# Four kv heads per tile instead of two in a one-token attention and MLP kernel

## The chip, the cores and the metric

The kernel runs on one core of one Trainium2 chip. The metric is device microseconds of one execution; the figure that counts is the median of the runs. A core has five engines with queues of their own: TensorE (PE, with its weight load PEld), VectorE (DVE), ScalarE (ACT), GpSimd (POOL) and SyncE (SP), which here issues nearly all transfers. Sixteen DMA engines move the data from HBM (the chip's main memory) to SBUF (on-chip, 128 partitions). TensorE writes to PSUM, eight banks of 128 partitions by 512 float32 elements.

## What is computed

One token `x` (576 values) passes through two branches that a gate mixes:

```python
# A: attention of 32 query heads on 16 kv heads, the last W = 4096 rows of the cache
q = (x @ wq).reshape(B, Sq, 32, 128).transpose(0, 2, 1, 3)
k = repeat(k_cache[:, :, Sk - W:, :], 2, axis=1)       # Sk = 32768
v = repeat(v_cache[:, :, Sk - W:, :], 2, axis=1)
p = softmax(einsum("bhqd,bhkd->bhqk", q, k) * 128**-0.5)
a = einsum("bhqk,bhkd->bhqd", p, v).transpose(0, 2, 1, 3).reshape(B, Sq, 4096) @ wo
# B: dense layer, F = 4608
b = gelu(x @ w1 + b1) @ w2 + b2
g = sigmoid((x * gate_w).sum(-1, keepdims=True))
out = g * a + (1 - g) * b
```

Everything is bfloat16 in HBM. Read are 16.8 MB of keys, 16.8 MB of values, 4.7 MB each of `wq` and `wo`, and 5.3 MB each of `w1` and `w2`: 53.6 MB in all. With one token, no datum is used twice.

## The kernel before

**Tiles of keys and values.** A tile holds two kv heads, interleaved on the partitions: head 2m on the even, head 2m + 1 on the odd partitions. Each partition holds 64 consecutive rows of its head, 16 KB in one piece (`load_kv`, L99; two transfers of 1 MB each, issued by SP). The pool `kv_pool` has six such buffers, used in turn by K tiles, V tiles and, at the end, the four groups of `w2`. A second pool of three buffers, `w_pool`, takes `wq` (two pieces), `w1` (three pieces) and `wo` (two).

**Units.** Work is counted in 16 units `h`. A unit is 32 chunks of a K tile, a chunk being the 128 rows that lie at one place of all partitions: half a tile. For each unit:

- `transposes(h, i)`, i from 0 to 7: four 128x128 matmuls with the identity turn four chunks (L233) into a PSUM tile `tp` (three banks, pool `ps_t`), and one copy puts them into `kT` (two buffers): VectorE at i = 0, 3, 6 (L242), ScalarE otherwise (L244).
- `scores(h, s)`, s = 0, 1: four matmuls of 512 columns, which run beside each other in four column groups of the array (L264). Their stationary columns are taken from `qz`, the queries of both heads padded with zeros. As a chunk mixes the keys of two heads, each query row also gets scores against the other head's keys.
- `values(h, i)`: four of them (i from 0 to 3, or 4 to 7) run side by side in four column groups (L340). Each has 32 stationary columns of `ez` (the probabilities, transposed, at zeros elsewhere) and 512 columns of V, and sums into `acc`.

**Softmax** (`softmax(b)`, L272) is made four times, for a block of four units each. `row_max` (L283) adds a mask that drops the scores against the other head and takes the maximum of each row; `turn_max` brings the maxima of a query together; `spread` gives them back to all rows and takes the exponential (L305); `put` transposes the probabilities (L313) and copies them into `ez` (eight VectorE copies, L318). `heads_out(b)` takes the four diagonal blocks out of `acc` (L352, L356) and turns the result (L363).

**Order.** It is written out by hand (a manual schedule: each engine takes its instructions in program order). The main loop (L547 to L585) runs over the units. In unit h, SP is given a K tile or a V tile, the transposes of unit h + 1 run, the scores of unit h between them, the steps of the last block's softmax one by one between these, and the values of unit h - 6. So up to the last block every softmax runs beside transposes and scores of the next. After the loop the last softmax runs between values (L596 to L612). `w1` is multiplied in three pieces (L452), its GELU spread over a unit (`gelu`, L462: `h_r`, nine `turn_h` with the small `hT` matmuls L479, and `act`).

**The end.** With all heads out, `ot`, `ow_ps`, `ow_m` and `ow` (L631 to L648) prepare the columns for `wo`. The blocks of four matmuls at L669 first go through `wo` (64 matmuls), then through the first three groups of `w2` (18 each), into `part`. L677 adds the bias; L688 sums the four column groups and the fourth group of `w2`, which is loaded in three pieces; L701 and L702 write the result.

**SP's queue.** SP issues in program order. A load waits for the buffer that it overwrites (the transposes or values that read it), and for the transfer eight issues earlier.

Of the kernel before, what the change touches and what calls it, by code (L numbers as in the profile page):

```python
# [16 lines left out]
def kernel(  # L17
# [24 lines left out]
    NCK = W // (P // 2)  # L42
    NCH = NCK // 2
    NU = 2 * (Hkv // 2)
# [19 lines left out]
    HB = 4  # L64
    NB = Hkv // HB
    R = 2 * HB
    RP = R // 2
    BC = 4
    NBL = NCH // BC
    NGR = 2 * NBL // NQ  # L70
    MASK = -1.0e30
# [5 lines left out]
    kv_pool = ctx.enter_context(tc.tile_pool(name="kv_pool", bufs=6))  # L77
# [20 lines left out]

    def load_kv(cache, m, name):  # L99
        t = kv_pool.tile([P, NCK, Dh], BF16, name=name, tag="kv")  # L100
        for e in range(2):
            nc.sync.dma_start(  # L102
                out=t[e:P:2],
                in_=cache[0, 2 * m + e, Sk - W : Sk, :].rearrange("(p c) d -> p c d", c=NCK),
            )
        return t
# [7 lines left out]
    WMAX = 36 * 256  # L114
# [17 lines left out]
    k_tiles[0] = load_k(0)  # L132
# [4 lines left out]
    for i in range(2):  # L137
        wq_t.append(load_flat(wq_flat, i * QP * QC, QP * QC, "wq_t"))

# [7 lines left out]
    qz = const.tile([P, Hkv // 2, 56], BF16, name="qz")  # L147
# [17 lines left out]
    for o in range(2):  # L165
# [21 lines left out]

    row_e = const.tile([P, 2], FP32, name="row_e")
    nc.vector.tensor_reduce(
        out=row_e[:], in_=ident_f[:].rearrange("p (a e q) -> p e a q", e=2, q=2), axis=AX.XY,  # L190
        op=ALU.add,
    )
    nc.vector.tensor_scalar(
        out=row_e[:], in0=row_e[:], scalar1=-MASK, scalar2=MASK, op0=ALU.mult, op1=ALU.add
    )
    mask = const.tile([P, BC * P], BF16, name="mask")
    for e in range(2):
        nc.vector.tensor_copy(
            out=mask[:, e::2], in_=row_e[:, e : e + 1].to_broadcast([P, BC * P // 2])
        )  # L200
# [27 lines left out]
    def transposes(h, i):  # L228
        if i == 0:
            kT[h] = kT_pool.tile([P, W], BF16, name="kT", tag="kT")  # L230
        tp = ps_t.tile([P, BC * P], FP32, name="tp", tag="tp")
        for c in range(BC):
            nc.tensor.matmul(  # L233
                tp[:, c * P : (c + 1) * P],
                lhsT=k_tiles[h // 2][:, (h % 2) * NCH + i * BC + c, :],
                rhs=ident[:],
                start=True,
                stop=True,
            )
        dst = kT[h][:, i * BC * P : (i + 1) * BC * P]  # L240
        if i in (0, 3, 6):
            nc.vector.tensor_copy(out=dst, in_=tp[:])  # L242
        else:
            nc.scalar.copy(out=dst, in_=tp[:])  # L244
# [4 lines left out]

    ez = const.tile([P, 2, HB // 2, 2 * NBL, BC, R], BF16, name="ez")  # L250
    nc.gpsimd.memset(ez[:].rearrange("p a b c d e -> p (a b c d e)"), 0.0)
# [4 lines left out]
    def scores(h, s):  # L256

        b, ul = h // HB, h % HB
        if ul == 0 and s == 0:
            s_tiles[b] = ps_s.tile([P, BC * P], FP32, name="s_ps", tag="s")  # L260
        lo = R * (NGR - 1 - 2 * (h % 2) - s)
        for t in range(NQ):
            i = 4 * s + t
            nc.tensor.matmul(  # L264
                s_tiles[b][32 * t : 32 * (t + 1), :],
                lhsT=qz[:, h // 2, lo : lo + 32],
                rhs=kT[h][:, i * BC * P : (i + 1) * BC * P],
                start=(ul == 0 and s == 0),
                stop=(ul == HB - 1 and s == 1),
            )  # L270

    def softmax(b):  # L272
# [3 lines left out]
        ms = small.tile([P, BC * P], FP32, name="ms", tag="ms")  # L276
        m8 = small.tile([1, R], FP32, name="m8", tag="m8")
# [4 lines left out]
        def row_max():  # L282
            nc.vector.tensor_tensor_reduce(  # L283
                out=ms[:], in0=s_ps[:], in1=mask[:], scale=1.0, scalar=-3.0e38,
                op0=ALU.add, op1=ALU.max, accum_out=mx[:],
            )

        def turn_max():
# [3 lines left out]
                out=m8[:], in_=mT[:].rearrange("o (s r) -> o r s", r=R), axis=AX.X, op=ALU.max  # L292
            )
            nc.vector.tensor_copy(
                out=m_all[:].rearrange("o (s r) -> o s r", r=R),
                in_=m8[:].rearrange("o (s r) -> o s r", s=1).to_broadcast([1, P // R, R]),
            )

        def spread():
# [6 lines left out]
                out=pr[:], in_=ms[:], func=ACT.Exp, bias=nb[:, 0:1], scale=SCALE,  # L306
# [3 lines left out]
        def put():  # L310
# [5 lines left out]
            for m in range(HB // 2):  # L316
                for s in range(NGR):
                    nc.vector.tensor_copy(  # L318
                        out=ez[:, b % 2, m, NQ * s : NQ * (s + 1), :, RP * m : RP * (m + 1)],
                        in_=pT[:].rearrange("p c (t s r) -> p t c s r", t=NQ, r=R)[  # L320
                            :, :, :, s, RP * m : RP * (m + 1)
                        ],
                    )
# [7 lines left out]
    def values(h, i):  # L331

        b, ul = h // HB, h % HB
        if ul == 0 and i == 0:

            pool, tag = (ps_t, "tp") if b == NB - 1 else (ps_o, "o")
            acc[b] = pool.tile([P, BC, Dh], FP32, name="acc", tag=tag)
        ct = i % NQ
        n = (h % 2) * NBL + i
        nc.tensor.matmul(  # L340
            acc[b][32 * ct : 32 * ct + 4 * R, :, :],
            lhsT=ez[:, b % 2, ul // 2, n, :, :].rearrange("p c r -> p (c r)"),
            rhs=v_tiles[h // 2][:, n * BC : (n + 1) * BC, :],
            start=(ul == 0 and i < NQ),
            stop=(ul == HB - 1 and i >= NBL - NQ),
        )
# [70 lines left out]
    qT = ps_m.tile([P, QC // Dh, 2, NB], FP32, name="qT", tag="m")  # L417
# [10 lines left out]
    for m in range(HB // 2):  # L428
        lo = R * (NGR - 1) + RP * m
        nc.vector.tensor_copy(  # L430
            out=qz[:, m :: HB // 2, lo : lo + RP],
            in_=qT[:, :, m, :].rearrange("p i b -> p b i"),
        )


    PIECES = [(0, 4), (4, 8), (8, 9)]
    U = F // 2
    h_box = []

    def w1_load(i):  # L440
        lo, hi = PIECES[i]
        return load_flat(w1_flat, lo * U, (hi - lo) * U, "w1_t")

    def w1_mul(i, w):
        lo, hi = PIECES[i]
        if i == 0:
            h_box.append(ps_a.tile([P, 2, 512], FP32, name="h_ps", tag="a"))
        for m in range(lo, hi):
            for k in range(2):
                for t in range(NQ):  # L450
                    off = (m - lo) * U + t * FC + k * FB
# [61 lines left out]
    def norm():  # L513

        sg = const.tile([P, NB, R], FP32, name="sg")
        nc.vector.tensor_tensor(
            out=sg[:],
            in0=sums[:].rearrange("p (b o) -> p b o", o=1).to_broadcast([P, NB, R]),
            in1=m_r[:].rearrange("p (o r) -> p o r", o=1).to_broadcast([P, NB, R]),
# [21 lines left out]


    W1_AT = {1: 0, 5: 1, 9: 2}
    LAG = HB + 2
    chain, tail, mlp = [], [], []
    w1_ready = None
    for h in range(NU):  # L547
        if 1 <= h < NU - 3 and h % 2 == 1:
            k_tiles[(h + 3) // 2] = load_k((h + 3) // 2)
        if h >= HB and h % 2 == 0:  # L550
            v_tiles[(h - HB) // 2] = load_v((h - HB) // 2)
        if h == 1:

            for o in range(2):
                nc.sync.dma_start(
                    out=b1_r[o : o + 32 * (NQ - 1) + 1 : 32],
                    in_=B_b1.rearrange("(o t k n) -> o t k n", o=2, t=NQ, k=2)[o],
                )
        w1_next = (W1_AT[h], w1_load(W1_AT[h])) if h in W1_AT else None
        for i in range(NBL):  # L560
            if 1 <= h < NU - 1:
                transposes(h + 1, i)

            at = (4, 6) if h % HB == 0 else (2, 5)
            if i in at:
                scores(h, at.index(i))
            if i in (0, 1, 3, 6) and chain:
                chain.pop(0)()
            if i in (0, 5) and tail:
                tail.pop(0)()  # L570
            for f in (mlp[0:1], mlp[1:4], mlp[4:7], mlp[7:10], mlp[10:11])[i] if i < 5 else []:
                f()
            if h >= LAG and i % 4 == 3:
                for j in range(i - 3, i + 1):
                    values(h - LAG, j)
        if h >= LAG and (h - LAG) % HB == HB - 1:
            tail = heads_out((h - LAG) // HB)
        mlp = []
        if w1_ready is not None:
            w1_mul(*w1_ready)  # L580
            if w1_ready[0] == len(PIECES) - 1:
                mlp = gelu()
        w1_ready = w1_next
        if h % HB == HB - 1 and h < NU - 1:
            chain = softmax(h // HB)  # L585


    row_max, turn_max, spread, put = softmax(NB - 1)
    for h in (NU, NU + 2):
        v_tiles[(h - HB) // 2] = load_v((h - HB) // 2)  # L590

    def unit(h):
        for i in range(NBL):
            values(h, i)

    row_max()  # L596
    unit(NU - LAG)
    turn_max()
    unit(NU - LAG + 1)
    spread()  # L600
    put()
    take, turn_out = heads_out(NB - 2)
# [132 lines left out]
```

## Time and profile before

| | |
|---|---|
| time, median of 3 runs | 135.0 us (134.98 to 135.0) |
| profiled execution | 136.33 us |
| its span, first to last instruction | 134.3 us |
| mean granted TensorE clock | 0.853 |
| bytes moved, mean rate over the span | 53.79 MB, 400 GB/s |
| busy: PE / DVE / ACT | 68% / 45% / 36% |
| chain of work that ended last | DMA 74%, PE 15%, DVE 6% |

The span is the stretch that the profiler records; the profiled execution's own time is 2.03 us longer, and profiled it is 1.3 us above the median. A granted clock of 1.00 is TensorE's full speed. In the chain of waits each piece of time is given to what the next step waited for. The rows used most, of the costliest groups (line, engine, operation, out<-in, shapes, count, then busy us and mean ns of one):

```profile
L244 ACT CAST kT<-tp 128x512 bf16<-128x512 f32 x80 | 44.1, 587 | 42.6 <-PE tp L233 42.3
L242 DVE CAST kT<-tp 128x512 bf16<-128x512 f32 x48 | 33.0, 690 | 36.9 <-PE tp L233 32.6
L233 PE MATMUL tp<-ident,k_t 128*128 128x128 bf16 x512 | 46.3, 242 | 4.5 <-DMA k_t<-in_A_k_cache_dram 2.9
L340 PE MATMUL acc<-v_t,ez 128*32 128x512 bf16 x128 | 13.1, 453 | 2.4 <-DVE a_s L356 2.1
```

A matmul's duration holds its way through the array, and matmuls overlap: 512 of 242 ns are busy for 46.3 us only.

### The profile page before, as it was taken

The numbers are of one execution on the slowest core, as the hardware profiler recorded it, in microseconds if no ns is written. First come the engines' busy times: TensorE is split into PE (matmuls) and PEld (weight loads), VectorE is DVE, ScalarE is ACT, GpSimd is POOL, SyncE is SP. The second block draws the span as 40 slices with busy tenths as digits, with TensorE's granted clock in tenths as the row PEclk, the third lists the DMA queues.
The fourth block names the chain that finished last, engine by engine and source line by source line (L and its number), as shares of the span: only waits on it lengthen the run. The fifth ranks groups of instructions, "written<-read, shape, count | busy, mean of one in ns | idle before, by whom it ended". The sixth has DMA issues, their size and how long they took to land.

```text
span 134.3 us, 2686 instructions
## 1 busy us (share of the span) xinstructions
PE 90.8 (68%) x1127; PEld 58.1 (43%) x1127; DVE 60.2 (45%) x165; ACT 48.6 (36%) x91; POOL 5.2 (4%) x11
## 2 busy tenths in 40 slices
PE   0007985298296899397898769969969365585370
PEld 0007941265264665254565447636644141342140
DVE  4934642135127665135486544476665544400020
ACT  3003660058136787136558411557751200000000
POOL 8700000000000000000000000000000000000000
PEclk9999999959959999959999995589999965558655
DMA  3999999999999999999999999999999999999930
GB/s 78 435 431 412 406 440 444 424 448 417 426 424 429 429 449 419 412 434 424 432 420 420 434 444 420 439 424 429 434 424 429 403 436 423 422 440 423 408 128 0
DMA packets 4809, 53.79 MB, mean 400 GB/s; under 512 B 819, under 2 KB 958, under 8 KB 1342
## 3 DMA queue, kind: packets, MB, share of 16 engines
q1 hardware_dynamic: 4792, 53.62, 94.5%
q8 instruction: 9, 0.15, 0.4%
q14 instruction: 2, 0.02, 0.0%
q10 hardware_dynamic: 6, 0.00, 0.0%
HBM read 53.62 MB, written 0.00 MB: 399 GB/s over the span
## 4 chain that ended last, share of the span: by engine, by line
DMA 74%; PE 15%; DVE 6%; SPq 1%; issue 1%; DVEq 0%
DMA w_t<-in_B_w_dram 48%; DMA v_t<-in_A_v_cache_dram 17%; DMA wq_t<-in_A_wq_dram 9%; PE tp L233 6%; PE acc L340 2%; DVE kT L242 2%; PE hT L479 2%; PE s_ps L264 2%; PE y_ps L688 1%; PE part L669 1%; SPq L102 1%; DVE a_s L356 1%; DVE ez L318 1%; DVE part_s L677 1%; DVE h_r L470 1%
## 5 line engine op out<-in xcount | busy, mean ns | idle before, releaser
L244 ACT CAST kT<-tp 128x512 bf16<-128x512 f32 x80 | 44.1, 587 | 42.6 <-PE tp L233 42.3
L242 DVE CAST kT<-tp 128x512 bf16<-128x512 f32 x48 | 33.0, 690 | 36.9 <-PE tp L233 32.6
L233 PE MATMUL tp<-ident,k_t 128*128 128x128 bf16 x512 | 46.3, 242 | 4.5 <-DMA k_t<-in_A_k_cache_dram 2.9
L233 PEld LDWEIGHTS <-k_t 128*128 128x128 bf16 x512 | 35.9, 109 | 17.8 <-issue 17.1
L340 PE MATMUL acc<-v_t,ez 128*32 128x512 bf16 x128 | 13.1, 453 | 2.4 <-DVE a_s L356 2.1
L264 PE MATMUL s_ps<-kT,qz 128*32 128x512 bf16 x128 | 13.7, 423 | 0.3 <-DVE qz L430 0.3
L669 PE MATMUL part<-w_t,gt 128*1 128x288 bf16 x54 | 4.0, 384 | 4.3 <-DMA w_t<-in_B_w_dram 4.3
L452 PE MATMUL h_ps<-w_t,x 128*32 128x288 bf16 x72 | 3.1, 310 | 4.8 <-DMA w_t<-in_B_w_dram 4.8
L677 DVE SCALAR_TENSOR_TENSOR part_s<-b_r,omg,part 128x576 f32<-128x576 bf16 x1 | 0.8, 812 | 12.2 <-PE part L669 12.2
L371 PE MATMUL x_ps<-x,dup 64*128 64x9 bf16 x1 | 0.2, 163 | 8.9 <-DMA x<-in_A_x_dram 8.9
L340 PEld LDWEIGHTS <-ez 128*32 128x32 bf16 x128 | 3.7, 102 | 5.7 <-issue 3.5
L264 PEld LDWEIGHTS <-qz 128*32 128x32 bf16 x128 | 3.3, 94 | 3.9 <-issue 1.0
L669 PEld LDWEIGHTS <-gt 128*1 128x1 bf16 x54 | 2.0, 99 | 6.3 <-issue 5.1
L669 PE MATMUL part<-wo_t,ow 128*1 128x288 bf16 x64 | 4.0, 443 | 1.0 <-DVE ow L647 1.0
L452 PEld LDWEIGHTS <-x 128*32 128x32 bf16 x72 | 2.1, 99 | 5.5 <-issue 5.3
L356 DVE SCALAR_TENSOR_TENSOR a_s<-acc,m_c,a_s 128x128 f32<-128x128 f32 x12 | 4.2, 351 | 0.4
L305 ACT ACTIVATE pr<-ms,nb 128x512 bf16<-128x512 f32 x4 | 2.9, 722 | 4.1 <-DVE nb L302 4.1
L318 DVE COPY ez<-pT 128x64 bf16<-128x64 bf16 x32 | 3.6, 183 | 1.5 <-PE pT L313 1.3
L363 PE MATMUL o_ps<-m_r,a_s 128*128 128x8 f32 x8 | 1.7, 290 | 3.2 <-DVE a_s L356 3.2
L479 PE MATMUL hT<-sel_f,h_r 128*64 128x4 f32 x36 | 2.7, 265 | 1.3 <-DVE h_r L470 1.3
L363 PEld LDWEIGHTS o_ps<-m_r,a_s 128*128 128x128 f32 x8 | 1.4, 219 | 4.9 <-DVE a_s L356 2.5
L290 PE MATMUL mT<-ident_f,mx 128*1 128x128 f32 x4 | 1.1, 270 | 3.2 <-DVE mx L283 3.2
(82 smaller groups left out, 52.5 us busy)
## 6 DMA issues: line engine op xcount, KB each, us to landing
k_t<-in_A_k_cache_dram SPq DMA_DIRECT2D x16, 1024.0 KB, 18.5
v_t<-in_A_v_cache_dram SPq DMA_DIRECT2D x16, 1024.0 KB, 17.6
wq_t<-in_A_wq_dram SPq DMA_DIRECT2D x2, 2304.0 KB, 14.2
w_t<-in_B_w_dram SPq DMA_DIRECT2D x2, 2304.0 KB, 21.6
wo_t<-in_A_wo_dram SPq DMA_DIRECT2D x2, 2304.0 KB
w_t<-in_B_w_dram SPq DMA_DIRECT2D x3, 1296.0 KB, 23.8
w_t<-in_B_w_dram SPq DMA_DIRECT2D x1, 864.0 KB
w_t<-in_B_w_dram SPq DMA_DIRECT2D x1, 576.0 KB, 18.3
```

The costliest lines, as they stand in the source:

```text
L233: nc.tensor.matmul(tp[:, c * P : (c + 1) * P], lhsT=k_tiles[h // 2][:, (h % 2) * NCH + i * BC + c, :], rhs=ident[:], start=True, stop=True,)
L242: nc.vector.tensor_copy(out=dst, in_=tp[:])
L244: nc.scalar.copy(out=dst, in_=tp[:])
L264: nc.tensor.matmul(s_tiles[b][32 * t : 32 * (t + 1), :], lhsT=qz[:, h // 2, lo : lo + 32], rhs=kT[h][:, i * BC * P : (i + 1) * BC * P], st ...
L305: nc.scalar.activation(out=pr[:], in_=ms[:], func=ACT.Exp, bias=nb[:, 0:1], scale=SCALE, accum_out=sums[:, b : b + 1],)
L318: nc.vector.tensor_copy(out=ez[:, b % 2, m, NQ * s : NQ * (s + 1), :, RP * m : RP * (m + 1)], in_=pT[:].rearrange("p c (t s r) -> p t c s ...
L340: nc.tensor.matmul(acc[b][32 * ct : 32 * ct + 4 * R, :, :], lhsT=ez[:, b % 2, ul // 2, n, :, :].rearrange("p c r -> p (c r)"), rhs=v_tiles ...
L356: nc.vector.scalar_tensor_tensor(out=a_s[:], in0=acc[b][:, c, :], scalar=m_c[:, c : c + 1], in1=a_s[:], op0=ALU.mult, op1=ALU.add,)
L363: nc.tensor.matmul(o_ps[:], lhsT=a_s[:], rhs=m_r[:], start=True, stop=True)
L452: nc.tensor.matmul(h_box[0][32 * t : 32 * (t + 1), k, 0:FB], lhsT=x2[:, m, :], rhs=w[:, off : off + FB], start=(m == 0), stop=(m == NM - 1),)
L479: nc.tensor.matmul(box[0][64 * e : 64 * (e + 1), j, :], lhsT=rows[:, j : j + RJ * 63 + 1 : RJ], rhs=sel_f[:, e, :], start=True, stop=True,)
L669: nc.tensor.matmul(part[32 * t : 32 * t + 1, k, 0:DB], lhsT=col, rhs=w[:, i * D + k * DB : i * D + (k + 1) * DB], start=(n == 0), stop=(n ...
```

## The change

- A tile holds **four** kv heads: head 4m + g on the partitions 4i + g. Each partition holds 128 consecutive rows, 32 KB in one piece; a tile is loaded by four transfers of 1 MB, one per head (`fill`). There are four K tiles and four V tiles of 4.2 MB, and `kv_pool` has three buffers of twice the size. The first K tile is loaded in two halves, `wq` between them. A unit is now a quarter of a tile.
- The copies out of `tp` sort the heads: they read with a step of four elements and write runs of 32, so that `kT` holds each head's keys by themselves. The scores of a head then meet only its own keys; the mask goes, and `row_max` is a plain maximum over PSUM.
- Softmax is made twice, for two tiles (eight units) each. The transposed probabilities are copied to SBUF by ScalarE (`pT_s`), repeated for four heads by four matmuls with `spr` (512 columns each, into three banks of `ps_t` and the bank of `acc`), and eight VectorE products with `m_g` keep each partition's own head on the way to `ez`.
- The order is written by tile: keys of tiles 0 and 1, softmax 0, values 0, first half of `w1`, keys of tile 2, values 1, second half of `w1`, keys of tile 3 with the `hT` matmuls among the first unit's transposes, softmax 1, values 2 and 3, end. The steps of a softmax follow each other, with nothing of other units between. `w1` comes in two pieces instead of three.
- `w2`'s four groups take two buffers, two groups each; the third group is loaded in two pieces (rows 0 to 4, 5 to 8).

```diff
-    kv_pool = ctx.enter_context(tc.tile_pool(name="kv_pool", bufs=6))
+    kv_pool = ctx.enter_context(tc.tile_pool(name="kv_pool", bufs=3))
...
+    def fill(t, cache, m, lo, hi):
+        for g in range(GH):
+            src = cache[0, GH * m + g, Sk - W : Sk, :].rearrange("(p c) d -> p c d", c=NCK)
+            nc.sync.dma_start(out=t[g:P:GH, lo:hi, :], in_=src[:, lo:hi, :])
...
-        dst = kT[h][:, i * BC * P : (i + 1) * BC * P]
+
+        dst = kT[h][:, :, i * BC : (i + 1) * BC, :].rearrange("d g c p -> d c g p")
+        tp = tp[:].rearrange("d (c p g) -> d c g p", c=BC, g=GH)
...
         def row_max():
-            nc.vector.tensor_tensor_reduce(
-                out=ms[:], in0=s_ps[:], in1=mask[:], scale=1.0, scalar=-3.0e38,
-                op0=ALU.add, op1=ALU.max, accum_out=mx[:],
-            )
+            nc.vector.tensor_reduce(out=mx[:], in_=s_ps[:], axis=AX.X, op=ALU.max)
...
-            for m in range(HB // 2):
-                for s in range(NGR):
-                    nc.vector.tensor_copy(
...
+            pT_s = small.tile([P, BC * P], BF16, name="pT_s", tag="pT_s")
+            nc.scalar.copy(out=pT_s[:], in_=pT[:].rearrange("p k n -> p (k n)"))
...
+            wide = []
+            for c in range(BC):
+                wide.append(spread_to[c].tile([P, BC * P], FP32, name="wide", tag=tags[c]))
+                nc.tensor.matmul(
+                    wide[c][:],
+                    lhsT=spr[:, PH * c : PH * (c + 1), :].rearrange("k i g -> k (i g)"),
+                    rhs=pT_s[:],
...
+            for m in range(NM2):
+                for c in range(BC):
+                    nc.vector.tensor_tensor(
+                        out=ez[:, m, :, c, :].rearrange("p (G k) r -> p k G r", k=BC),
...
+    def tile_keys(m):
+
+        for h in range(4 * m, 4 * m + 3):
+            if h > 0:
+                for i in range(NBL):
+                    transposes(h + 1, i)
+                    if i in (2, 5):
+                        scores(h, i // 3)
+            else:
+                unit_scores(h)
+        unit_scores(4 * m + 3)
...
+    tile_keys(0)
+    tile_turn(1)
+    tile_keys(1)
+    k_tiles[2] = load_k(2)
+
+    for f in softmax(0):
+        f()
+    take, turn_out = heads_out(0)
+    tile_values(0)
     take()
-    unit(NU - HB)
+    w1_mul(0, w1_a)
+    turn_out()
+    v_tiles[1] = load_v(1)
+    w1_b = w1_load(1)
+
+    tile_turn(2)
+    tile_keys(2)
+    k_tiles[3] = load_k(3)
+
+    take, turn_out = heads_out(1)
+    tile_values(1)
+    take()
+    w1_mul(1, w1_b)
+    turn_out()
+    v_tiles[2] = load_v(2)
+    mlp = gelu()
+    mlp.pop(0)()
+    for i in range(NBL):
+        transposes(12, i)
+        for f in (mlp[0:2], mlp[2:4], mlp[4:6], mlp[6:8], mlp[8:9], mlp[9:10], [], [])[i]:
+            f()
+    tile_keys(3)
+    v_tiles[3] = load_v(3)
+
+    for f in softmax(1):
+        f()
+    take, turn_out = heads_out(2)
+    tile_values(2)
+    take()
+    tile_values(3, (0, 1))
     turn_out()
     norm()
     sums_start()
...
+    tile_values(3, (2, 3))
+    take, turn_out = heads_out(3)
     take()
     turn_out()
...
+        if g % 2 == 0:
+            t = kv_pool.tile([P, 2, NCK // 2 * Dh], BF16, name="w2_t", tag="kv")
+        w2_t.append(t[:, g % 2, :])
+        cut = {NG - 2: (0, 5, RJ), NG - 1: (0, 6, 8, RJ)}.get(g, (0, RJ))
```

## The prediction, made before the result was known

> **What bounds the kernel now.** First the page: busy shares, then the 40 slices.
>
> ```profile
> span 134.3 us, 2686 instructions
> PE 90.8 (68%) x1127; PEld 58.1 (43%) x1127; DVE 60.2 (45%) x165; ACT 48.6 (36%) x91; POOL 5.2 (4%) x11
> ...
> DMA  3999999999999999999999999999999999999930
> ...
> HBM read 53.62 MB, written 0.00 MB: 399 GB/s over the span
> ```
>
> No engine passes 68%; the transfers are busy in every slice from 3.4 us to the end. The chain of waits agrees (74% of the span is DMA). Next the table of stretches, for the rate of each stage (columns: stretch, its length, busy us and instructions of PE, PEld, DVE, ACT, POOL, then granted clock, DMA share, GB/s).
>
> ```profile
> 10.00:20.00 10.00, 8.52 (x88) 6.94 (x92) 5.01 (x11) 5.61 (x11) 0.00 (x0) 1.00 0.99 423
> 20.00:30.00 10.00, 6.03 (x68) 3.42 (x68) 2.33 (x5) 2.15 (x4) 0.00 (x0) 0.83 1.02 432
> 80.00:90.00 10.00, 8.77 (x91) 6.00 (x91) 5.25 (x16) 3.54 (x7) 0.00 (x0) 0.66 0.99 423
> 115.00:120.00 5.00, 4.03 (x72) 2.36 (x72) 1.02 (x3) 0.00 (x0) 0.00 (x0) 0.50 1.02 431
> ```
>
> 10 to 20 us is mostly wq (18 KB rows), 20 to 30 keys (16 KB rows), 115 to 120 mostly wo and w2 (9 to 10 KB rows): 423, 432, 431 GB/s. The rate does not follow packet size. Summing the stretches gives the clock of bytes that I use below: 7.31 MB at 20 us, 11.63 at 30, 33.09 at 80, 52.3 at 125. Last the timeline of the end (start, length, engine, line, operation, count, idle before).
>
> ```profile
> 102.08 0.69 DVE L283 CUSTOM_DVE_ANT_0 ms<-s_ps,mask 128x512 f32<-128x512 f32 x1 [0.60 <-PE s_ps L264]
> ...
> 105.94 0.61 PE L340 MATMUL acc<-v_t,ez 128*32 128x512 bf16 x8 [0.28 <-DVE ez L318]
> ...
> 109.42 2.75 PE L340 MATMUL acc<-v_t,ez 128*32 128x512 bf16 x24
> ...
> 116.28 4.01 PE L669 MATMUL part<-wo_t,ow 128*1 128x288 bf16 x64 [0.97 <-DVE ow L647]
> ...
> 120.77 1.55 PE L669 MATMUL part<-w_t,gt 128*1 128x288 bf16 x18 [0.48 <-DMA w_t<-in_B_w_dram]
> ...
> 123.86 0.90 PE L669 MATMUL part<-w_t,gt 128*1 128x288 bf16 x18 [1.54 <-DMA w_t<-in_B_w_dram]
> ...
> 126.99 1.60 PE L669 MATMUL part<-w_t,gt 128*1 128x288 bf16 x18 [2.24 <-DMA w_t<-in_B_w_dram]
> ...
> 128.63 0.81 DVE L677 SCALAR_TENSOR_TENSOR part_s<-b_r,omg,part 128x576 f32<-128x576 bf16 x1 [12.20 <-PE part L669]
> ```
>
> This decides the case. The data is the bound, but with little to spare: before its three waits for w2, TensorE idles 0.48 + 1.54 + 2.24 = 4.3 us. Work that reaches wo later than 116.28 by more than 4.3 us moves the end.
>
> **The transfers: no gain.** The bytes are the same, and up to each milestone the order sums to the same: 35.2 MB up to the last keys (before: K pairs 0 to 7, V 0 to 3, wq, w1; after: K0 to K3, V0, V1, wq, w1), wo and w2 last. 32 KB packets instead of 16 buy nothing by the three rates above. Half the partitions per transfer is not in the trace; the nearest step is 128 (423) to 64 (432), no loss. I take 430 GB/s, bounds 3% either way.
>
> The Trainium skill ("DMA: Bandwidth & Descriptors", Rules for kernel authors) asks for 128 partitions and at least 1 MiB per transfer; K and V keep 1 MiB but have 32 partitions. The 432 of the 64-partition keys speaks against its partition half; by that rule the sum would grow as in rival 3.
>
> Starvation: buffers are now 4.2 MB and three, so a load waits for a whole four-head tile. K2 waits for K0's transposes (about 34 us) with V0 and w1 in flight until 49; V1 for K1 (about 49) with K2 in flight until 59; V2 for K2 (about 77) with K3 until 85; w2's second half for values 2 (about 117) with wo and w2's first half until 122. Cover is 5 to 15 us each time; below 5, a slip costs its excess.
>
> **Covered edits.** Setup on VectorE grows by about 1 us (spr: half of turn's 2.17; m_b, m_4, m_g 0.8; less row_e and mask, 1.0), and VectorE idles from 7.0 to 9.2, waiting for x. Two more qz copies (0.17 each) delay the first scores at 22.5; the next keys land at 25.9. SP has two more issues of 0.65 before x; x lands behind 2.1 MB anyway. Two softmaxes instead of four take work from engines under 50% busy. Scores stay 128 matmuls, values 128, w1 72. Cutting w2's third group at row 5 leaves 10 of 18 matmuls behind the last of it: 0.6 us, only if the data still ends it.
>
> **The path that decides**, on the span's clock. Two TensorE speeds matter. A row of four 512-column matmuls takes 0.62 us on the timeline after idle time and 0.40 later; the change comes 5.3 us after work starts at 26.0, 4.5 us after 36.1 and 4.8 us after 56.3; at 79 to 88, among the small hT matmuls, it takes over 8.
>
> The Trainium skill ("TensorE: Matmul & The Clock Gate", HAM oscillation) says the array falls to half clock after about 3.4 us of idling; the granted clock of 0.50 at 115 to 120 agrees in direction. The new softmax holes are longer than that. Without the slow speed steps 5 and 7 would be some 4 us shorter, and the data would end it as in rival 1.
>
> 1. K3 complete: 35.2 MB is at 85.0 by the byte clock. Landing lags it: 25.9 for 8.91 MB (23.7), 77.0 for 31.0 MB (75.1), 126.95 for w2's third group (125.0). I add 2: 87.0. What stands ahead on TensorE: K1 lands at 35.2, four units of 3.4 (step 3) and the last scores end at 49.7; softmax 8.6 (step 4); values, w1, turn_out 5.7: 64.0. K2 landed at 61; four units and scores: 78.5; values 1, w1, turn_out 4: 82.5. So the last tile's transposes start at 87.0, cold.
> 2. Its first unit carries the hT matmuls: 32 transposes at 0.12 (8 in 1.03 us at 85.07) + three hT rows of 0.89 = 6.6: 93.6. Before, two units followed the load that ends at 35.2 MB; now four.
> 3. Three units of 32 transposes and 8 scores: 28 transposes and 8 scores took 3.0 us (47.75 to 50.76), so 3.4 each, 0.6 more while cold: 104.4. Last scores wait for the last copies: 105.4. The copies read PSUM in steps of four elements; ScalarE's 587 ns (L244) has no such row. VectorE's L291 reads PSUM in steps of eight, 128 elements in 278 ns, against 280 for L203 on SBUF; I take no loss, with 10% less and double as ends (rival 2).
> 4. Softmax, now with TensorE's queue holding only itself, values behind it. Row maximum to transposed probabilities is 3.6 us (102.08 to 105.66); then the added copy 0.59 (a ScalarE 128x512 row), the first spreading matmul 0.6 (128 rows by 512 columns, cold), eight VectorE products at 0.425 (the 128x256 tensor_tensor, L639; ends 0.35 and 0.69), waits 0.4: 8.6, where before it is 3.9 to the first values matmul. acc shares its bank with the last spread tile, so values wait for all eight: 114.0.
> 5. values(2): 8 rows of four at 0.43 (24 matmuls in 2.75): 3.4. values(3), first half: 1.7, the take beside it. turn_out and norm 1.3 (108.10 to 109.42). Second half warm: 0.9. Total 121.3. Before, only 32 matmuls were left after the last softmax; now 64.
> 6. From last values to wo 4.1 (112.17 to 116.28, same code): 125.4, against 116.28.
> 7. wo 4.0 again cold (129.4); w2's three groups have landed and run without waiting, 18 steps of four columns (six took 1.55 slow and 0.90 fast above): four at 0.24, the rest at 0.13, 2.8: 132.2, where before it is 128.6 (part_s starts 128.63). The rest (5.7 us) is the same code.
>
> Sum: +3.6 us. Check: 9.1 later at wo, less 4.3 of absorbed waiting, less 1.2 of clock. The profiled execution is 136.33 us around a span of 134.3, 1.3 above the median 135.0; the difference is added to the median: **138.6 us**. All rows at the slow end (units 4.4, g's 1.45) give +9; at the fast end (first unit 4.9, units 3.2, values and wo at half) wo starts near 120 and the data ends it.
>
> **Rivals.** (1) *Faster: the data keeps the end.* If steps 2 to 6 come out over 4.3 us shorter, w2's landing (126.95) sets the end and its cut gives 0.6 back: 134.4. The deciding point is TensorE reaching wo at about 121. For: VectorE and ScalarE are half idle, and a 5 us run warms the array. Against: the 8.6 us hole does not overlap anything. 0.14. (2) *Strided copies are slower.* ScalarE paces a unit (5 copies at 0.54 to 0.59). Double costs 2.9 per unit, 12 on the last tile, and the loads starve as well: about 150; at 20% more it is +2.4, 141. 0.10. (3) *32-partition transfers run slower.* 3% on the 25 MB of K and V that precede K3's end costs 1.8 on every later step, 140.4; 6% 142.2. Against: the 64-partition rows. 0.08. (4) *It doesn't do what it says*: packets double, the data ends no earlier, and the tail slips by only what the waits absorb: 134.8 to 135.2. 0.04. The forecast has 0.64.
>
> Faster by over 0.2% (0.27 us, about what a measurement here can tell from none): 0.14; within: 0.04; slower: 0.82. The range leaves out the top of rivals 2 and 3 and the fast half of rival 1: 134.6 to 142.0.
>
> **What would show it.** Right: GB/s still 420 to 435; TensorE idle over 6 us twice between last scores and first values; wo's first matmul after 123; no wait for w2 at the second and third group. Step 1: last key tile's first transpose at 86 to 88. Step 3: copies at 587 and 690 ns. Wrong: TensorE waits for w2 before the third group; a DMA slice below 9 before 120 us; copies far from 587; a tile's keys taking under 13 or over 20 us.

## The result and the profile after

The changed kernel is slower: 140.64 us, median of 6 runs (139.75 to 141.67), against 135.0 (134.87 to 135.07); ratio 1.0415, 95% interval 1.0375 to 1.0455. The forecast was 138.6 us, in a range of 134.6 to 142.0. Ratios here leave out executions more than 1.5% above the fastest of the same kernel; only `wq_first`, below, has any (five of twelve, which its median and its range still hold).

The page of the changed kernel: span, busy shares, granted clock and DMA by slice (3.45 us each), and the queue that carries nearly all data (packets, MB, share of 16 engines).

```profile
span 137.9 us, 2644 instructions
PE 91.8 (67%) x1121; PEld 59.8 (43%) x1121; DVE 62.3 (45%) x139; ACT 48.2 (35%) x89; POOL 4.4 (3%) x11
...
PEclk9999999559999995559999999555599955599599
DMA  4999999999999999999999999999998999999300
...
q1 hardware_dynamic: 3960, 53.62, 92.0%
```

The queue held 4792 packets and 94.5% of 134.3 us before; now 3960 packets and 92.0% of 137.9 us: 126.9 us both times, so larger packets changed nothing in it. But the last digits of the DMA row are 300: the transfers end at about 129 us, as before, and 9 us of work follow them. The slices with a clock of 5 lie at 24 to 31 us, behind the two softmaxes, at the last key tile and at `wo`. Then the timeline of the changed kernel (start, length, engine, line, operation, count, idle before), cut to the path that decides:

```profile
87.38 0.59 PE L247 MATMUL tp<-ident,k_t 128*128 128x128 bf16 x4 [4.89 <-DMA k_t<-in_A_k_cache_dram]
...
107.96 0.69 DVE L300 TENSOR_REDUCE mx<-s_ps 128x1 f32<-128x512 f32 x1 [0.61 <-PE s_ps L281]
...
113.01 3.03 DVE L347 TENSOR_TENSOR ez<-wide,m_g 128x256 bf16<-128x256 f32 x8 [2.77 <-PE wide L338]
116.09 4.75 PE L373 MATMUL acc<-v_t,ez 128*32 128x512 bf16 x48 [1.84 <-DVE ez L347]
...
127.32 3.60 PE L715 MATMUL part<-wo_t,ow 128*1 128x288 bf16 x64 [0.97 <-DVE ow L693]
130.76 2.37 PE L715 MATMUL part<-w_t,gt 128*1 128x288 bf16 x54
133.17 0.81 DVE L723 SCALAR_TENSOR_TENSOR part_s<-b_r,omg,part 128x576 f32<-128x576 bf16 x1 [5.69 <-PE part L715]
```

TensorE waits 4.89 us for the last key tile (first line); after that no step of this path waits for data. All 54 `w2` matmuls run in one piece, where before three waits for `w2` stood between them. `wo` begins at 127.32 instead of 116.28. The copies that now sort the heads cost what the plain ones did (587 and 690 ns before):

```profile
L260 ACT CAST kT<-tp 128x512 bf16<-128x512 f32 x80 | 43.9, 587 | 46.4 <-PE tp L247 45.8
...
L258 DVE CAST kT<-tp 128x512 bf16<-128x512 f32 x48 | 32.5, 689 | 36.0 <-PE tp L247 31.7
```

### The profile page after: what moved, and what is told of

Read it like the earlier page. It is cut to its first block, busy times and chain, and to the rows that moved or that the text cites. A ratio compares the mean times of both kernels' runs of the same rounds, so it can differ in the third digit from the quotient of the medians.

```text
span 137.9 us, 2644 instructions
## 1 busy us (share of the span) xinstructions
PE 91.8 (67%) x1121; PEld 59.8 (43%) x1121; DVE 62.3 (45%) x139; ACT 48.2 (35%) x89; POOL 4.4 (3%) x11
## 3 DMA queue, kind: packets, MB, share of 16 engines
q1 hardware_dynamic: 3960, 53.62, 92.0%
## 4 chain that ended last, share of the span: by engine, by line
DMA 42%; PE 30%; DVE 12%; ACT 8%; issue 4%; SPq 1%; ACTq 0%; DVEq 0%
DMA k_t<-in_A_k_cache_dram 31%; DMA wq_t<-in_A_wq_dram 11%; PE tp L247 11%; ACT kT L260 6%; PE acc L373 5%; PE part L715 4%; DVE kT L258 4%; PE s_ps L281 3%; DVE ez L347 2%; PE hT L511 2%; PE wide L338 2%; DVE a_s L389 2%; SPq L105 1%; ACT pr L320 1%; DVE mx L300 1%
## 5 line engine op out<-in xcount | busy, mean ns | idle before, releaser
L247 PE MATMUL tp<-ident,k_t 128*128 128x128 bf16 x512 | 46.8, 244 | 13.8 <-DMA k_t<-in_A_k_cache_dram 7.9
L247 PEld LDWEIGHTS <-k_t 128*128 128x128 bf16 x512 | 36.5, 110 | 24.7 <-issue 23.7
L281 PE MATMUL s_ps<-kT,qz 128*32 128x512 bf16 x128 | 13.7, 417 | 1.7 <-ACT kT L260 1.4
L373 PE MATMUL acc<-v_t,ez 128*32 128x512 bf16 x128 | 11.3, 516 | 3.7 <-issue 1.9
L373 PEld LDWEIGHTS <-ez 128*32 128x32 bf16 x128 | 4.3, 122 | 10.4 <-issue 6.8
L347 DVE TENSOR_TENSOR ez<-wide,m_g 128x256 bf16<-128x256 f32 x16 | 6.0, 420 | 5.6 <-PE wide L338 5.6
L385 DVE TENSOR_SCALAR a_s<-acc,m_c 128x128 f32<-128x128 f32 x4 | 1.4, 351 | 9.8 <-PE acc L373 9.8
L338 PE MATMUL wide<-pT_s,spr 128*128 128x512 bf16 x8 | 3.7, 622 | 1.3 <-ACT pT_s L332 1.3
L153 DVE CAST ident_f<-ident 128x128 f32<-128x128 bf16 x1 | 3.3, 3254 | 1.8 <-POOL ident masks.py:199 1.8
L320 ACT ACTIVATE pr<-s_ps,nb 128x512 bf16<-128x512 f32 x2 | 1.4, 687 | 5.8 <-DVE nb L317 5.8
L511 PEld LDWEIGHTS hT<-sel_f,h_r 128*64 128x64 f32 x36 | 2.6, 212 | 1.0 <-issue 1.0
```

Source lines behind the costliest of these rows:

```text
L153: nc.vector.tensor_copy(out=ident_f[:], in_=ident[:])
L247: nc.tensor.matmul(tp[:, c * P : (c + 1) * P], lhsT=k_tiles[h // 4][:, (h % 4) * NCH + i * BC + c, :], rhs=ident[:], start=True, stop=True,)
L281: nc.tensor.matmul(s_tiles[b][32 * g : 32 * (g + 1), :], lhsT=qz[:, m, g, lo : lo + 32], rhs=kT[h][:, g, s * CG : (s + 1) * CG, :], start= ...
L338: nc.tensor.matmul(wide[c][:], lhsT=spr[:, PH * c : PH * (c + 1), :].rearrange("k i g -> k (i g)"), rhs=pT_s[:], start=True, stop=True,)
L347: nc.vector.tensor_tensor(out=ez[:, m, :, c, :].rearrange("p (G k) r -> p k G r", k=BC), in0=wide[c][:].rearrange("p (k r m G) -> p m k G ...
L373: nc.tensor.matmul(acc[m][32 * ct : 32 * ct + 4 * R, :, :], lhsT=ez[:, m % NM2, n, :, :].rearrange("p c r -> p (c r)"), rhs=v_tiles[m][:, ...
```

## The experiments

**Theory:** the end left the transfers and hangs on the chain of work that starts when the last key tile lands. **Rivals:** the four-head transfers are slower or starve; the tail had no room before either; only the length of the hole matters, not TensorE's speed behind it. Times are compared with runs of the kernel before on the same chip (medians 134.94 to 135.13).

### hT_early

```diff
-    mlp.pop(0)()
+    for f in mlp:
+        f()
     for i in range(NBL):
         transposes(12, i)
-        for f in (mlp[0:2], mlp[2:4], mlp[4:6], mlp[6:8], mlp[8:9], mlp[9:10], [], [])[i]:
-            f()
```

> The changed kernel with one thing moved: the nine hT steps and the GELU run before the last key tile's transposes, in the 4.89 us in which TensorE waits for that tile. Theory (the end hangs on the chain from the last key tile's landing): the first unit, 7.5 us in the changed kernel (87.38 to 94.85), needs about 4.5; the scores end 2.5 to 3.5 us earlier, and so does wo's first matmul (124 to 125), and the time falls by 2.5 to 3.5 us, to about 137.5. Rival (the transfers are slower or starve): nothing in the transfers changes, so the time stays within 0.5 us.

Measured: 135.67 us, ratio 1.0041 (1.0018 to 1.0063). 36 small matmuls and the GELU steps behind them, moved by a few microseconds, take back 5.0 of the 5.6 us. The edit touches no transfer; SP's first issue for `w2` comes 5.4 us earlier (101.42 instead of 106.87), as its buffer is free earlier, but in neither profile does a `w2` matmul wait for its data. Its timeline:

```profile
87.38 5.05 PE L247 MATMUL tp<-ident,k_t 128*128 128x128 bf16 x44 [2.34 <-DMA k_t<-in_A_k_cache_dram]
...
92.37 0.40 PE L281 MATMUL s_ps<-kT,qz 128*32 128x512 bf16 x4
...
102.51 0.69 DVE L300 TENSOR_REDUCE mx<-s_ps 128x1 f32<-128x512 f32 x1 [0.62 <-PE s_ps L281]
...
122.14 4.01 PE L714 MATMUL part<-wo_t,ow 128*1 128x288 bf16 x64 [0.97 <-DVE ow L692]
```

The changed kernel has this at the same place:

```profile
98.62 0.62 PE L281 MATMUL s_ps<-kT,qz 128*32 128x512 bf16 x4
...
101.10 0.40 PE L281 MATMUL s_ps<-kT,qz 128*32 128x512 bf16 x4
```

The tile lands at the same time, to the hundredth; the scores end 5.45 us earlier, and so `wo` begins 5.2 earlier. That is more than the 3.5 expected. The hT matmuls themselves take 3.0 us of TensorE (four times 0.65 and 0.41); the rest is speed and waiting. With the hT matmuls among the transposes, a row of four score matmuls still takes 0.62 us at 98.62 and 0.40 only at 101.10, 13.7 us after the landing; here it takes 0.40 at 92.37, after 5.0. So the second unit is faster too.

### warm_hole

```diff
-    for f in softmax(1):
+    keep_warm(3)
+    for f, n in zip(softmax(1), (3, 4, 0, 7)):
         f()
+        keep_warm(n)
```

`keep_warm(n)` issues n matmuls of 512 columns into a bank that nothing reads.

> The changed kernel with 17 matmuls of 512 columns added that nothing reads, in TensorE's queue between the steps of the last softmax. Theory (part of the loss is the slow TensorE speed after the hole): the 48 values matmuls behind it, 4.75 us, take 2.7; wo may gain another 1; the softmax itself stays at 8.1 or grows by up to 0.4. Time 2 to 3 us lower, about 138. Rival (only the hole's length matters): the time stays or grows by up to 0.5 us.

Measured: 139.02 us (138.15 to 140.11), ratio 1.0286 (1.0214 to 1.0358). By the ratios that is 1.4 us under `after_again` (below, 140.61, 1.036 to 1.0415; the intervals just miss each other), less than expected. Two lines of its timeline (of its longest execution, 140.11):

```profile
116.89 2.94 PE L373 MATMUL acc<-v_t,ez 128*32 128x512 bf16 x48
...
126.83 4.01 PE L726 MATMUL part<-wo_t,ow 128*1 128x288 bf16 x64 [0.97 <-DVE ow L704]
```

The 48 values matmuls take 2.94 us instead of 4.75, as expected, but the last added matmuls let them begin 0.6 later against the scores' end. Counted from the scores' end, `wo` begins 0.7 us earlier than in the changed kernel. There `wo` is slow (4.01 us, against 3.60 and 3.85 in the changed kernel's two profiles); why is not shown. So the slow speed behind the hole is a part of the loss, and adding work repairs some of it; with four runs, and a profiled execution no faster than the changed kernel's first (139.75), its size is not well known. The Trainium skill ("TensorE: Matmul & The Clock Gate", HAM oscillation) says to keep TensorE from idling longer than about 3.4 us; the 4.75 against 2.94 agrees only in direction, because in the changed kernel's softmax no single wait of TensorE is longer than 1.84 us: it works 3.1 of 8.2 us, in short pieces, and is slow all the same.

### before_late_1 and before_late_2

The kernel before, with VectorE products ahead of `ez` in the last softmax (12, and 24):

```diff
+            if b == NB - 1:
+                late = const.tile([P, 256], FP32, name="late")
+                for _ in range(12):
+                    nc.vector.tensor_tensor(
+                        out=late[:], in0=ms[:, 0:256], in1=ms[:, 256:512], op=ALU.mult
+                    )
```

> The kernel before with 12 VectorE products of 128x256 added in the last softmax, between the transposed probabilities and ez; nothing reads them. They delay everything behind the last softmax by 4 to 5 us. Theory (the kernel before has 4.3 us of waiting for w2 behind wo that absorb a late start of wo): the time grows by 0 to 0.7 us. Rival (the tail has no room): it grows by all of the delay, 4 to 5 us.

> The same with 24 products, a delay of 8 to 10 us. Theory: the time grows by the delay less the 4.3 us of absorbed waiting, 4 to 5.5 us, much like the changed kernel, whose wo starts 11.0 us later in the profiles. Rival (no room): it grows by 8 to 10 us.

Measured: 136.02 us, ratio 1.0059 (1.0027 to 1.0092), and 141.26, ratio 1.0448 (1.039 to 1.0506). The products run for 5.46 and 10.96 us, but their first 1.5 us lie beside the exponential and the transposes, which VectorE would have waited for anyway. This is the longer one:

```profile
103.59 0.69 DVE L283 CUSTOM_DVE_ANT_0 ms<-s_ps,mask 128x512 f32<-128x512 f32 x1 [0.60 <-PE s_ps L264]
...
105.80 10.96 DVE L319 TENSOR_TENSOR late<-ms 128x256 f32<-128x256 f32 x24
...
116.67 0.87 DVE L324 COPY ez<-pT 128x64 bf16<-128x64 bf16 x8
```

From the row maximum to `wo` it is 14.2 us in both profiles of the kernel before, 18.4 with 12 products and 23.9 with 24: delays of 4.2 and 9.7 us, as expected. The time grows by 0.8 and 6.0 us by the ratios, so the tail of the kernel before absorbs 3.4 and 3.7 us and passes on the rest. Profile against profile (the table below, from `before_again`), `wo` begins 5.9 and 9.6 us later and the executions are 1.5 and 5.3 us longer: 4.3 to 4.4 absorbed, as forecast. The longer delay gives the kernel before the changed kernel's time, and its tail:

```profile
127.45 4.01 PE L675 MATMUL part<-wo_t,ow 128*1 128x288 bf16 x64 [0.97 <-DVE ow L653]
131.24 2.53 PE L675 MATMUL part<-w_t,gt 128*1 128x288 bf16 x54
```

The growth of 6.0 us lies above the 5.5 that were the upper end: by the medians the tail absorbs somewhat less than 4.3.

### softmax_per_tile and softmax_per_tile_hT_late

A softmax for each tile: half of the rows of the score bank are zeros then, four products instead of eight write `ez`. Between `row_max`, `turn_max` and `spread` of softmax m stand the values of tile m - 1. In the first kernel hT runs ahead of the last tile's transposes, in the second among them.

```diff
+        row_max()
+        if mv is not None:
+            tile_values(mv, (0, 1))
+        turn_max()
+        if mv is not None:
+            tile_values(mv, (2, 3))
...
-            for m in range(NM2):
+            for m in (b % NM2,):
```

> The changed kernel with the hT matmuls early (as in hT_early) and a softmax for each four-head tile instead of each two: four softmaxes, each with four VectorE products instead of eight; values of tile m - 1 stand in TensorE's queue inside softmax m, so only the 32 values matmuls of the last tile are left after the last softmax. Theory (the end hangs on the work after the last key tile lands): from hT_early's wo start at 122.1, softmax 1.7 shorter, values of tile 2 (3.6) and one take (1.5) off the path: wo at 115 to 117, the waits for w2 return, the data ends it. Time 134.2 to 135.0, at or just under the kernel before, with w2's cut third group saving up to 0.6. Rival (four-head tiles and 32 KB packets cost time by themselves): it stays at 135.7 or above, as in hT_early.

> The same with the hT matmuls back among the first transposes of the last key tile, so that the softmax per tile is tried alone against the changed kernel. Theory: the last keys end 4 to 5 us later than in softmax_per_tile, wo at 119 to 122, inside the slack; time 134.5 to 135.5. If the hT position alone explains the loss, it stays near the changed kernel's 140.

Measured: 135.68 us, ratio 1.0043 (1.0029 to 1.0056), and 135.67, ratio 1.0032 (1.0006 to 1.0059). Each of the two repairs, moving hT or splitting the softmax, brings the changed kernel back to within 0.6 us of the kernel before; both together bring no more. With one repair `wo` begins at 122.1, and the `w2` matmuls of the first three groups still run in one piece; with both the data ends it again. In the timeline of softmax_per_tile the waits for `w2` are back (its third group is cut, nine matmuls a part):

```profile
120.10 3.74 PE L718 MATMUL part<-wo_t,ow 128*1 128x288 bf16 x64 [0.97 <-DVE ow L696]
...
125.70 0.53 PE L718 MATMUL part<-w_t,gt 128*1 128x288 bf16 x9 [0.40 <-DMA w_t<-in_B_w_dram]
127.15 0.54 PE L718 MATMUL part<-w_t,gt 128*1 128x288 bf16 x9 [0.92 <-DMA w_t<-in_B_w_dram]
```

That is where the theory expected it, but not its time: 134.2 to 135.0 was expected, and no version was faster than the kernel before. `wo` also began 3 us later than expected. Most of that comes before the softmax: the scores end at 105.1 us instead of hT_early's 102.5, since the hT matmuls still run until 88.0 there and the transposes then wait for VectorE until 90.76. And one softmax still costs 7.4 us (105.19 to 112.62). In softmax_per_tile_hT_late the scores end 2.7 us later than in softmax_per_tile, not 4 to 5, and `wo` begins at 122.13, where 119 to 122 was expected.

### before_again and after_again

> The kernel before, unchanged, for a second profile: the first one was 1.3 us above the median. Expected: a span of about 133.0 for a time of about 135.0, with the missing 1.3 us in the tail behind the last w2 data (part_s to the end 5.7 in the first profile, at a granted clock of 0.5). If the 1.3 us lie in the transfers instead, the last w2 data land earlier than 126.95.

> The changed kernel, unchanged, for a second profile and times beside the others: median 140 to 141, and a profile that is up to 1.5 us longer than the first. If the spread of 1.9 us comes from when TensorE reaches full speed, the additional time lies in matmul stretches after the last key tile's landing (first unit, values, wo), and the landing stays at 87.4 within 0.5.

Measured: one execution of the kernel before, 135.27 us with a span of 133.2; and for the changed kernel 140.61 (139.85 to 140.76), ratio 1.0388 (1.036 to 1.0415), profiled at 140.76 with a span of 138.7. The second profile of the kernel before differs in the tail:

```profile
126.52 0.90 PE L669 MATMUL part<-w_t,gt 128*1 128x288 bf16 x18 [2.27 <-DMA w_t<-in_B_w_dram]
127.45 0.81 DVE L677 SCALAR_TENSOR_TENSOR part_s<-b_r,omg,part 128x576 f32<-128x576 bf16 x1 [9.46 <-PE part L669]
```

The third `w2` group takes 0.90 us, where the first profile has 1.60, and lands at 126.52 instead of 126.99. So the first profile, the one predicted from, caught the slow TensorE speed at its third group: 0.7 of its 1.1 us; the other 0.4 are transfers, as the second half of the expectation would have it. From `part_s` to the end it is 5.7 and 5.8 us, so the tail, where the expectation looked first, holds none of it. In the changed kernel's second profile the landing is 0.4 later (87.80), first unit and values as slow as in the first (values 5.10), and `wo` begins at 127.95. Its 0.8 us more are half landing, half values and `wo`.

### wq_first and half_rows

`wq_first` loads x and `wq` ahead of the first key tile, which is then loaded whole. `half_rows` splits every load, so that packets are 16 KB and transfers 0.5 MB again:

```diff
-        fill(t, cache, m, 0, NCK)
+        for lo in (0, NCK // 2):
+            fill(t, cache, m, lo, lo + NCK // 2)
```

> softmax_per_tile with x and wq loaded first and the first key tile whole behind them (no half rows); transposes of units 0 and 1 follow q on TensorE. It tests what is left between the four-head kernels and the kernel before (0.5 to 0.6 us). By the bytes of the first 10 us the four-head profiles move 2.84 to 2.95 MB and the two of before 3.08 and 3.10, 0.2 MB or 0.5 us late from the start, and no profile of theirs makes it up. Theory (the loss sits in loading half tiles at the start): 3.05 MB or more at 10 us, time 135.0 to 135.3, level with before. Rival (four heads per tile move slower all through, or the loss is in the tail): 135.6 to 135.9 as before.

> softmax_per_tile with every key and value load split in two, so that packets are 16 KB again and a transfer 0.5 MB; K0 is loaded as there. A direct test of the packet size, on a kernel that the data ends. Theory (the rate does not follow the packet size): within 0.4 us of softmax_per_tile, 135.3 to 136.1. Rival 1 (32 KB packets do save something that other losses hide): 136.5 or more. Rival 2 (half rows at a 32 KB pitch are what is slow in the first 10 us): 0.2 MB per 2.1 MB lost again and again, some 7 us, 142.

`half_rows`: 136.07 us, ratio 1.0069 (1.0049 to 1.0089), against 1.0043 (1.0029 to 1.0056) with 32 KB packets and 1 MB transfers. The two sizes together are worth about 0.4 us, 0.8 at most by the intervals, which overlap. Both rivals fall.

`wq_first` does not bear out its theory: 136.62 us (135.21 to 138.55, twelve runs), ratio 1.007 (1.0039 to 1.01). Its table of stretches sums to 2.95 MB at 10 us, no better, but to 7.34 at 20 us, level with the two profiles of before (7.31 and 7.35) and ahead of softmax_per_tile's 7.08; then it falls back (32.73 MB at 80 us against 33.01), and `wo` begins only at 125.37. That the keys of the first tile now start too late is a guess.

The same sums answer what the expectation says of the start. At 10 us the other four-head profiles have 2.77 to 2.95 MB, those with two heads 3.08 to 3.15. But at 100 us the difference is gone: 41.66 to 41.81 MB in the six four-head profiles with 1 MB transfers and the first tile in halves, 41.66 to 41.76 with two heads. From 100 to 110 us those six move 394 to 408 GB/s, and the two-head profiles 421 to 425: 0.13 to 0.31 MB, or 0.3 to 0.7 us at 430 GB/s. So what is left of the loss fits this stretch and not the start. `half_rows` moves 424 GB/s there, but is 0.3 to 0.4 MB behind at 100 us. The cause of either is open.

### All profiled executions together

| kernel | `wo` begins, us | time of this execution, us |
|---|---|---|
| before, first profile | 116.28 | 136.33 |
| half_rows | 117.34 | 136.44 |
| before_again | 117.84 | 135.27 |
| softmax_per_tile | 120.10 | 135.58 |
| softmax_per_tile_hT_late | 122.13 | 135.03 |
| hT_early | 122.14 | 135.48 |
| before_late_1 | 123.75 | 136.77 |
| wq_first | 125.37 | 137.89 |
| warm_hole | 126.83 | 140.11 |
| the changed kernel | 127.32 | 139.75 |
| before_late_2 | 127.45 | 140.60 |
| after_again | 127.95 | 140.76 |

Up to 122 us the time does not follow the start of `wo` (135.0 to 136.4 us; the two longest have a slow third group of `w2`, 1.60 us, and a slow last part of it, 0.89); from there it grows with it, about one for one, whether the kernel has two heads a tile or four. That is the theory in one table.

## Why the prediction was right

The mechanism was right: no gain from the transfers, absorbed waiting of some 4 us, a chain from the last key tile's landing that uses it up and more. By its steps:

| step | predicted | measured |
|---|---|---|
| 1 last key tile, first transpose | 87.0 | 87.38 |
| 2 first unit, with hT | 6.6 | 6.8 (to about 94.2, its 32nd transpose) |
| 3 three units and last scores | 11.8 | 13.7 (to 107.93) |
| 4 softmax to first values | 8.6 | 8.1 (to 116.09) |
| 5 values 2 and 3 | 7.3 | 7.4 (to 123.45) |
| 6 to `wo` | 4.1 | 3.9 (to 127.32) |
| 7 `wo` and three groups | 6.8 | 5.8 (to 133.14) |
| the rest | 5.7 | 4.8 |
| span | 137.9 | 137.9 |

- Steps 2 and 3 were 2.1 us too short, nearly all of it in step 3, which allowed 0.6 us for a cold TensorE. The last hT matmul ends at 92.8; at 98.62 TensorE is still slow. The prediction had read the kernel before as slow all through 79 to 88 us, "among the small hT matmuls". Its rows say otherwise:

```profile
80.50 0.40 PE L264 MATMUL s_ps<-kT,qz 128*32 128x512 bf16 x4
...
83.01 0.62 PE L340 MATMUL acc<-v_t,ez 128*32 128x512 bf16 x4
...
89.84 0.40 PE L340 MATMUL acc<-v_t,ez 128*32 128x512 bf16 x4
```

TensorE is fast behind the first twelve hT matmuls (granted clock 1.00 until 81 us), loses its speed among the others (0.50 from 82 to 87.5) and regains it about 5 us after the last of them. So the price of the hT matmuls was to be paid behind them, in step 3. Besides, VectorE takes a kT copy only behind the GELU's steps (94.92), and the next transposes wait 0.25 and 0.73 us for copies.

- Step 7 and the rest were 1.9 too long, both for the same reason: TensorE was fast again sooner than taken (`wo` with 3.60 instead of 4.01 us, the last 36 `w2` matmuls with 0.75 instead of 1.30). That errors of opposite sign gave the exact span is luck.
- **The mis-sized term** is the last one: the difference of spans (3.6) was "added to the median". The profile of before that it starts from was 1.1 us longer than before_again, most of it a slow third group; and the changed kernel's profile is its fastest run of six, 0.9 under its median. The shift between medians is 5.6 us. The prediction noted the 1.3 us by which that execution lies above its median and still took its span as the reference. Long executions recur: of the 59 of the kernel before that were timed beside the experiments, six took 135.8 to 136.1 us.
- Absorbed waiting: 4.3 us forecast; 3.4 and 3.7 by the ratios of before_late_1 and before_late_2, 4.3 to 4.4 by their profiles.
- Starvation: little. One slice has 8 for DMA, in the stretch from 100 to 110 us (share 0.95, 405 GB/s); 50.07 MB are in by 120 us, against 50.18 and 50.25 in the two profiles of before. The path does not wait for these bytes.
- Rival 1 (faster) fell with `wo` at 127.3 instead of 121. What it named as its condition is what softmax_per_tile makes true (120.1) and hT_early nearly (122.1), and both end at 135.7. Its time, 134.4, was not reached; by the sums under wq_first the bytes fall behind between 100 and 110 us by 0.3 to 0.7 us, about what w2's cut was to give back. That this is the cause is argued, not shown.
- Rival 2 (strided copies): 587 and 689 ns, no loss. Rival 3 (32 partitions): 424 to 450 GB/s in the stretches from 10 to 60 us. The Trainium skill's 128 partitions ("DMA: Bandwidth & Descriptors", Rules for kernel authors) are not needed at 1 MB a transfer in this kernel: 126.9 us of queue time with 64 and with 32.
- Three signs came out against the forecast although its mechanism held, so they were set too narrow. The last tile's keys took 20.5 us, over the 20 that were to speak against it, for the reasons of steps 2 and 3. A DMA slice lies below 9 before 120 us (the 8 above). And TensorE idles 5.1 us between last scores and first values, both times, not over 6: it works 3.1 and 3.3 us of the 8.2 and 8.4.

## What to carry to other kernels

In a kernel that the transfers bound, find the last load that real work still depends on, and sum what stands behind it; the idle waits at the end tell how much of that sum is free. Coarser tiles save nothing where the rate does not follow packet size, but put more work behind the last landing; whatever does not need that load (here 36 small matmuls and the GELU behind them, worth 5 us) belongs in the wait before it. And compare more than one profile before adding a difference of spans to a median.

## What the runs showed of the hardware that was not expected

- Small matmuls do not keep TensorE fast. In the kernel before, the speed is lost among the 36 hT matmuls (4 columns in float32, 0.65 us for 8) and comes back about 5 us behind them. In the changed kernel, full speed came about 12 us after the landing and 7 behind the last hT matmul (granted clock 0.50 until 99.2 us, 1.00 from 100); in softmax_per_tile, where the same matmuls end at 88.0 just ahead of the transposes, about 8 us behind them (0.50 until 96.0, with a wait of 1.4 us on the way); in hT_early, 5 us after the landing. Whether their size, their type or the pauses around them count was not tried.
- The changed kernel's first six runs spread by 1.9 us, the four of after_again by 0.9. The kernel before spreads by 0.2 us over six runs, but by 1.0 to 1.2 over 17 to 23. That an end on TensorE spreads the times more is not shown.
- Reading PSUM in steps of four float32 elements costs neither ScalarE nor VectorE anything (587 and 689 ns for 128x512).
- The same cast of `ident` (L146 before, L153 after) took 733 ns before and 3254 in the changed kernel, while copies behind it became faster (`dup` 1.7 to 0.21 us, `turn` 2.2 to 1.04). GpSimd fills buffers at that time in both. VectorE's setup ended at 8.5 us instead of 7.0, still ahead of x (9.48); the cause was not tried.
